# Attention, then two MLPs, on one core: block 0's first two pairs ahead of block 1, its x written from PSUM, and an order that knows the shared port

## The chip, the cores and the metric

The kernel runs on one core of a Trainium2 chip. TensorE multiplies, VectorE, ScalarE and GpSimd do the elementwise work, and SyncE issues all DMAs. The metric is the device time of the core in microseconds (us), the median of several runs of the whole kernel. Engine names in the rows: PE is TensorE's matmul, PEld its weight load, DVE VectorE, ACT ScalarE, POOL GpSimd, SPq SyncE's queue.

## The reference

All inputs and the result are float32 in shape, but the values need more than half precision: several inputs are drawn with factors of 8, q with 64.

```
# attention, 8 batches, 8 heads, 576 tokens, head size 64, 32 packed queries p per head
def sm_attn(qq, kk, vv):
    s = scale * qq @ kk.T; s = s - max(s); a = exp(s); a = a / (sum(a) + 1e-9); return a @ vv
p_packed = sm_attn(p, k, v)
out = sm_attn(q, p_packed, p_packed)
x = out, heads joined: 4608 tokens x 512
# first MLP, 512 -> 1536 -> 512
x = (silu(x @ w_gate) * (x @ w_val)) @ w_out
# second MLP, 512 -> 2048 -> 512
h = x @ w_in;  g = h if h >= 1, 0 if h <= -1, else (h + 1)**2 / 4
result = g @ w_out
```

The weights arrive as float64 words and are turned into float32 on the chip.

## The kernel before, in words

Precision comes from splitting: every float32 operand is scaled by a power of two and split into a float16 high part and a float16 low part, and each product is made as three float16 products (high x low, low x high, high x high). To save products, 2 x 2 blocks of quarters are multiplied by a scheme of Strassen's kind with seven products (P1 to P7). For that, sums and differences of quarters are made first (`sums`, `split_quarters`, line 501), on GpSimd or VectorE.

The work comes in these pieces:

- Attention goes by "quads" of four heads; two quads (0 and 1) make batch 0, quads 2 and 3 batch 1, and so on to 15. A quad has `load`, `stage_a` (scores of p against k, softmax), `stage_b` (transposes, values, norms and exponents of the packed heads), `stage_c` (scores of q, softmax) and `stage_d` (outputs, evacuated from PSUM, scaled and stored in the DRAM tensor `xT`). The last quad of a batch also makes `kx1`, an exponent for the batch's x.
- The tokens are cut into nine blocks of 512. Block 0 lies in batch 0; block 1 takes the last 64 tokens of batch 0 and most of batch 1. `load_x` (line 1187) brings a block's x in as two `raw` tiles, `split_x` scales and splits it and also stores the split form (`xsp`); `fetch_x` reads that form again when another pair needs it.
- The first MLP's hidden layer goes in six "pairs" of unit tiles. A unit (`first_unit`, 84 products of 256 columns at line 1110) makes one pair's hidden values for one block; the products with the output weights follow, at line 1248 for pairs 0 to 2 (`second_products`, 24 products of 512 columns per pair and block) and at line 1366 for the rest. The second MLP has eight units and the same two steps.
- `PHASES` (line 552) sets the order of units: pair 0 for blocks 0 and 1, pair 1 for blocks 0 and 1, pair 2 for blocks 0 and 1, then pairs 0 to 2 for the other blocks, then pairs 3 to 5 for all.
- Weights are converted (`convert_w1`, `prepare_w1`, `convert_chunk`, `prepare_w2`): the words are joined (`from_words`), the values are squared, a matmul with ones sums the squares over the partitions, VectorE takes the maximum over the columns, and from it come an exponent and a scale.

What sets the order of instructions is a planner written out in Python, the class `Order` (line 42). Each operation is registered with an estimated cost on every engine that can do it, its reads, writes and buffers. A simulation then picks, for each engine that is free, the waiting operation with the earliest due time ("late", from the order in which TensorE's work is registered) whose inputs are there and whose buffers can be had. TensorE's own work is taken nearly as registered, from a window of 32. The instructions are issued in that order; on the chip each engine works through its own list and waits where an input is missing. Buffers come from pools (38 `op`, 4 `raw`, 8 PSUM banks `ps`, 4 `h`), and those of the main pools are handed out in the order of registration. An operation marked `shared` is one that VectorE and GpSimd can't do at the same time, in the planner's model.

Around the first units, places (two per unit) say when what is registered: `NEXT` for the quads, `LATE` for the weights of pairs 1, 2 and so on, `CHUNKS` for those of the second MLP. `load(i)` takes two `op` buffers for k and two for v.

Of the kernel before, what the change touches and what calls it, by code (L numbers as in the profile page):

```python
# [9 lines left out]
F32 = mybir.dt.float32  # L10
# [32 lines left out]
class Order:  # L43
# [8 lines left out]
    PATIENCE = {"exp": 0.0}  # L52
    WINDOW = 32
# [72 lines left out]
    def run(self):  # L126
# [126 lines left out]
def packed_attention_then_two_mlps(ctx, tc, qT, kT, v, pT, w1, wo, w2, wo2, out):  # L253
# [52 lines left out]
    a2s = const.tile([128, 2 * U2], I32, name="a2s")  # L306
    top1 = const.tile([128, U1 + G1], F32, name="top1")
# [5 lines left out]
    kp = const.tile([128, B * NQUAD, 3], I32, name="kp")  # L313
# [187 lines left out]
    def split_quarters(raw, scale, op, key, left, wait_sum=0.0, wait_lo=0.0):  # L501
        base = lambda: raw.t[:, 0:4, :]
        copy(1024, base, base, q(raw, 0, 1, 2, 3) + [key], q(raw, 0, 1, 2, 3), scale=scale)
# [14 lines left out]
    def sums(raw, left, wait):  # L518
# [14 lines left out]
        (1, (0, 1), (0, 2)), (1, (1, 2), (0, 2)), (1, (2, 3), (0, 2)), (1, (0, 3), (2, NB)), (1, (3, 6), (0, NB)),  # L533
# [60 lines left out]

    def convert_w1(item):
# [3 lines left out]
        for src in srcs:  # L599
# [5 lines left out]
            for a, b in ((0, 512), (512, 1024)):  # L605
                wb = o.buf("h")
                n = b - a

                def words(wb=wb, n=n):
                    return wb.t.rearrange("p a b n -> p (a b n)").bitcast(I32).rearrange("p (n w) -> p n w", w=2)  # L610

                dma(n * 0.001, words,
                    lambda src=src, a=a, b=b: src[:, a:b].bitcast(I32).rearrange(
                        "p (n w) -> p n w", w=2),
                    [], [(wb, 0)])
                dst = lambda a=a, b=b, line=line: line()[:, a:b]
                from_words(words, dst, [(wb, 0)], q(raw, *range(a // N, (b - 1) // N + 1)), n)
# [4 lines left out]
    def prepare_w1(item):  # L622
        kind, p = item
        raws = st.pop(("w1", item))
        ps = o.buf("ps")

        def norm():
            for u, (_, sq) in enumerate(raws):
                s = sq()
                if kind == "out":  # L630
                    moving, dst = [s[:, 0:4:3, :], s[:, 1:3, :]], ps.t
                else:
                    moving = [m[:, :, h:h + 128] for m in (s[:, 0:4:3, :], s[:, 1:3, :])
                              for h in (0, 128)]
                    dst = ps.t[:, u * 256:u * 256 + 256]
                for m, mv in enumerate(moving):
                    nc.tensor.matmul(dst, ones, mv, start=(m == 0), stop=(m == len(moving) - 1))  # L637

        pe(0.43 * len(raws), norm, [k for raw, _ in raws for k in q(raw, 4, 5)], [(ps, 0)],
           unit=ps, opens=True)  # L640
        i = p if kind == "in" else U1 + p
        dve(512, lambda: nc.vector.tensor_reduce(top1[:, i:i + 1], ps.t[:, :512], axis=AX.X, op=ALU.max),
            [(ps, 0)], [("top", 1, i)], 1.5, 0.0)
# [14 lines left out]
    def load(i):  # L658
        b, qd = divmod(i, NQUAD)
        pb = o.buf("pb")  # L660
        kt, vt = [o.buf("op") for _ in range(2)], [o.buf("op") for _ in range(2)]
# [7 lines left out]
        for j, c0, c1 in ((0, 0, 3), (1, 3, 4)):  # L669
            dma(0.2, lambda j=j, c0=c0, c1=c1: flat(vt[j], (c1 - c0) * 4 * D).rearrange(  # L670
                "p (c d) -> p c d", d=4 * D
            ), lambda c0=c0, c1=c1: v[b, 128 * c0:128 * c1, cols].rearrange("(c p) d -> p c d", p=128),
                [], [(vt[j], 0)])
        dma(0.1, lambda: flat(vt[1], 8 * D)[:S - 512, 4 * D:], lambda: v[b, 512:, cols],
            [], [(vt[1], 1)])
        st["in", i] = (kt, vt, pb)
# [28 lines left out]
    def stage_a(i):  # L705
        kt, vt, pb = st["in", i]
# [22 lines left out]
    def stage_b(i):  # L729
        b, qd = divmod(i, NQUAD)  # L730
        vt = st.pop(("in", i))[1]
# [24 lines left out]
        def values():  # L756
            for c, (off, n) in enumerate(CH):
                vc = flat(vt[c // 3], 768)[:n, (c % 3) * 4 * D:]
# [6 lines left out]
        pe(0.92, values, [(a1T, 0), (a1T, 1), (vt[0], 0), (vt[1], 0), (vt[1], 1)], [(pv, 0)],  # L765
# [58 lines left out]
        if qd == NQUAD - 1:  # L824
# [4 lines left out]
            field(lambda: kx1[:, b:b + 1], lambda: topx[:, b:b + 1], [("topx", b)], [("kx1", b)], 2.0)  # L829
        st[i] = (pp, parts, ppT)  # L830

    def stage_c(i):
# [33 lines left out]
        z2 = o.buf("op")  # L866
# [4 lines left out]
        copy(S, lambda: halves(0), lambda: flat(z, S), [(z, 0)], [(z2, 0)])  # L871
# [4 lines left out]
    def stage_d(i):  # L876
        b, qd = divmod(i, NQUAD)
        pp, parts, z2, halves = st.pop(i)
        for j in range(2):
            xs = o.buf("op")  # L880
            for u in range(2):
# [10 lines left out]
                copy(H2, lambda u=u, xs=xs: flat(xs, S)[:, u * H2:(u + 1) * H2],  # L892
                     lambda xo=xo: xo.t[:, :H2], [(xo, 0), ("kp", i, 2)], [(xs, u)], 1.0,
                     scale=lambda: kp[:, i, 2:3].bitcast(F32), psum=True)
            dma(0.3, lambda j=j: xT[:, 2 * qd + j, b * S:(b + 1) * S], lambda xs=xs: flat(xs, S),
                [(xs, 0), (xs, 1)], [("x", b, qd, j)], 10.0)
            if b == 0:
                st["xs", qd, j] = xs
# [233 lines left out]
    def convert_chunk():  # L1132
# [14 lines left out]
        square(512, sq, dst, q(b, "d"), q(b, "w"))  # L1147
        dma(0.25, lambda: w2f[:, i, 512 * h:512 * h + 512], dst, q(b, "d"), [("w2f", i, h)])
        t = o.buf("ps")
        n = 128 if i < U2 else 512  # L1150

        def norm():
            for m in range(512 // n):
                nc.tensor.matmul(
                    t.t[:, :n], ones, sq()[:, m * n:(m + 1) * n],
                    start=(m == 0), stop=(m == 512 // n - 1),
                )

        pe(0.25, norm, q(b, "w"), q(t, 0), unit=t, opens=True)

        dve(n, lambda: nc.vector.tensor_reduce(
            top2[:, i, h:h + 1], t.t[:, :n], axis=AX.X, op=ALU.max
        ), q(t, 0), [("top", 2, i, h)], 1.5, 0.0)
        if h == 1 and i % 2 == 1:

            j = i - 1
            dve(1, lambda: nc.vector.tensor_reduce(
                top2[:, j, 0:1], top2[:, j:j + 2, :], axis=AX.XY, op=ALU.max
            ), [("top", 2, j + u, c) for u in range(2) for c in range(2)], [("top", 2, j, 0)], None, 0.0)
# [17 lines left out]
    def load_x(layer, b):  # L1187
        src = {1: xT, 2: x2T}[layer]
        raws = []
        for kk in range(2):  # L1190
            raw = o.buf("raw")
            for kh, sl in ((0, slice(0, 2)), (1, slice(2, 4))):
                halves = lambda kk=kk, kh=kh: src[:, kk + 2 * kh, b * T:(b + 1) * T]
                if layer == 1 and b == 0:
                    xs = st.pop(("xs", kh, kk))
                    halves, r = lambda xs=xs: flat(xs, S)[:, :T], [(xs, 0), (xs, 1)]
                elif layer == 2:
# [9 lines left out]
    def split_x(layer, b, pw, raws):  # L1207
        out_ops = []
        for d, raw in enumerate(raws):
            op = operand()  # L1210
            split_quarters(raw, pw.x(), op, (pw.f, 0), False, SUM_WAIT, X_LO)
# [170 lines left out]
    def total(b):  # L1382
        t = o.buf("ps")
        pe(0.1, lambda: nc.tensor.matmul(t.t[:, :4], ones32, sq2[:, b, :]),
           [("sq2", b)], [(t, 0)], unit=t, opens=True)

        dve(4, lambda: nc.vector.tensor_reduce(
            topx[:, B + b:B + b + 1], t.t[:, :4], axis=AX.X, op=ALU.add
        ), [(t, 0)], [("topx2", b)], 2.0, 0.0)
# [210 lines left out]
    for k, (n, p) in enumerate(line):  # L1600
# [94 lines left out]
```

## Time and profile before

| | |
|---|---|
| runs | 1619.83, 1624.52, 1621.31 us, median 1621.31 |
| profiled execution | 1620.46 us, span 1618.7 us |
| mean granted clock of TensorE | 0.984 |
| DMA traffic | 308.60 MB on the program's queue |
| chain that ended last | PE 85%, DVE 7%, ACT 2%, issue 2%, POOL 2%, DMA 1% |

The span runs from the first to the last instruction. Busy times are sums over an engine's instructions; an idle time in brackets in a row of the timeline is the time the engine stood still ahead of the row, with the instruction that ended it.

### The profile page before, as it was taken

The numbers are of one execution on the slowest core, as the hardware profiler recorded it, in microseconds if no ns is written. First come the engines' busy times: TensorE is split into PE (matmuls) and PEld (weight loads), VectorE is DVE, ScalarE is ACT, GpSimd is POOL, SyncE is SP. The second block draws the span as 40 slices with busy tenths as digits, with TensorE's granted clock in tenths as the row PEclk, the third lists the DMA queues.
The fourth block names the chain that finished last, engine by engine and source line by source line (L and its number), as shares of the span: only waits on it lengthen the run. The fifth ranks groups of instructions, "written<-read, shape, count | busy, mean of one in ns | idle before, by whom it ended". The sixth has DMA issues, their size and how long they took to land.

```text
span 1618.7 us, 35291 instructions
## 1 busy us (share of the span) xinstructions
PE 1555.6 (96%) x13772; PEld 1290.2 (80%) x13772; DVE 1298.2 (80%) x2104; ACT 989.4 (61%) x1690; POOL 1167.4 (72%) x993
## 2 busy tenths in 40 slices
PE   4778999999999999999999999999999999999999
PEld 2446666776777778888888888888888888888888
DVE  8889998778675647889999899988777898775674
ACT  5767677677665456666666767666554556654541
POOL 5476556475464357778769989988788888886884
PEclk8779999999999999999999999999999999999999
DMA  8776967647337755666776853245433553244422
GB/s 295 244 268 234 334 223 238 199 170 236 133 140 250 265 179 194 233 249 234 262 238 207 303 190 128 102 150 189 160 105 121 186 182 119 102 170 160 150 60 79
DMA packets 147240, 310.86 MB, mean 192 GB/s; under 512 B 18560, under 2 KB 55424, under 8 KB 147072
## 3 DMA queue, kind: packets, MB, share of 16 engines
q1 hardware_dynamic: 147072, 308.60, 55.7%
q8 instruction: 108, 1.77, 0.4%
q14 instruction: 60, 0.49, 0.1%
HBM read 191.76 MB, written 115.74 MB: 190 GB/s over the span
## 4 chain that ended last, share of the span: by engine, by line
PE 85%; DVE 7%; ACT 2%; issue 2%; POOL 2%; DMA 1%; SPq 0%; POOLq 0%; DVEq 0%; ACTq 0%
PE ps L1110 46%; PE ps L1366 27%; PE ps L1248 7%; PE ps L697 2%; PE ps L886 1%; POOL op L364 1%; POOL raw L364 1%; DVE raw L364 1%; DVE raw L438 1%; DVE h L434 1%; DVE ps L1093 0%; ACT op L376 0%; DMA x2T<-acc 0%; DVE h L1093 0%; PE ps L637 0%
## 5 line engine op out<-in xcount | busy, mean ns | idle before, releaser
L1110 PE MATMUL ps<-op,op 128*128 128x256 f16 x7560 | 906.2, 273 | 7.0 <-DVE u L382 2.5
L1110 PEld LDWEIGHTS <-op 128*128 128x128 f16 x7560 | 737.7, 98 | 116.6 <-issue 14.5
L364 POOL TENSOR_TENSOR op<-h,op 128x512 f16<-128x512 f32 (+2 forms) x344 | 419.5, 1238 | 167.0 <-ACT op L376 140.6
L1366 PE MATMUL ps<-op,op 128*128 128x256 f16 x4158 | 513.3, 273 | 0.0
L1366 PEld LDWEIGHTS <-op 128*128 128x128 f16 x4158 | 406.7, 98 | 47.5 <-issue 0.3
L376 ACT CAST op<-h 128x512 f16<-128x512 f32 (+2 forms) x368 | 202.9, 591 | 92.0 <-POOL h L364 36.1
L364 POOL TENSOR_TENSOR raw<-raw 128x256 f32<-128x256 f32 (+1 forms) x169 | 156.2, 938 | 71.0 <-ACT raw L378 43.4
L364 POOL TENSOR_TENSOR h<-h,h 128x512 f32<-128x512 f32 (+1 forms) x160 | 197.9, 1237 | 11.9 <-DVE h L1488 4.3
L1485 ACT ACTIVATE ps<-m,half,f 128x512 f32<-128x512 f32 x144 | 112.3, 780 | 108.0 <-POOL m L1482 61.1
L378 ACT ACTIVATE p<-ps,f 128x512 f32<-128x512 f32 x174 | 118.8, 685 | 95.2 <-PE ps L1110 90.2
L1266 DVE SCALAR_TENSOR_TENSOR acc<-ps,f,acc 128x512 f32<-128x512 f32 x169 | 125.7, 744 | 58.6 <-PE ps L1366 55.8
L364 POOL TENSOR_TENSOR op<-raw,op 128x512 f16<-128x512 f32 (+3 forms) x100 | 157.3, 1593 | 15.7 <-ACT op L376 9.5
L1248 PE MATMUL ps<-op,op 128*128 128x512 f16 x648 | 155.4, 379 | 0.0
L1488 DVE SCALAR_TENSOR_TENSOR h<-ps,f,h 128x512 f32<-128x512 f32 x144 | 106.4, 742 | 32.5 <-ACT ps L1485 32.3
L1093 DVE SCALAR_TENSOR_TENSOR h<-ps,f,p 128x512 f32<-128x512 f32 x126 | 93.5, 743 | 42.5 <-PE ps L1110 37.2
L1248 PEld LDWEIGHTS <-op 128*128 128x128 f16 x648 | 63.0, 98 | 57.2 <-issue 0.9
L364 POOL TENSOR_TENSOR h<-h 128x512 f32<-128x512 f32 x57 | 78.1, 1371 | 26.0 <-DVE h L1457 15.3
L1482 POOL TENSOR_SCALAR m<-h,f 128x512 f32<-128x512 f32 x72 | 61.7, 856 | 48.6 <-ACT ps L1485 28.9
L364 DVE TENSOR_TENSOR op<-h,op 128x512 f16<-128x512 f32 (+1 forms) x79 | 96.7, 1234 | 0.0
L364 POOL TENSOR_TENSOR op<-op,t 128x576 f32<-128x576 f32 x32 | 39.9, 1246 | 71.9 <-DVE t L848 22.5
L378 ACT ACTIVATE u<-ps,f 128x512 f32<-128x512 f32 x87 | 59.6, 685 | 44.9 <-PE ps L1110 44.6
L376 ACT CAST op<-raw 128x512 f16<-128x512 f32 (+3 forms) x126 | 77.5, 655 | 13.9 <-DVE raw L364 6.9
(148 smaller groups left out, 1791.2 us busy)
## 6 DMA issues: line engine op xcount, KB each, us to landing
op<-xsp SPq DMA_DIRECT2D x88, 448.0 KB, 6.2
xsp<-op SPq DMA_DIRECT2D x72, 448.0 KB, 4.2
sums<-acc SPq DMA_DIRECT2D x88, 256.0 KB, 2.7
acc<-sums SPq DMA_DIRECT2D x88, 256.0 KB, 3.6
op<-wsp SPq DMA_DIRECT2D x44, 448.0 KB, 4.8
op<-wsp_out SPq DMA_DIRECT2D x38, 448.0 KB, 5.3
h<-in_w SPq DMA_DIRECT2D x24, 512.0 KB, 5.2
op<-in_kT SPq DMA_DIRECT2D x32, 288.0 KB, 5.3
```

The costliest lines, as they stand in the source:

```text
L364: lambda e: engine(e).tensor_tensor(dst(), x(), y(), op=op), r, w, late,
L376: nc.scalar.copy(dst(), src())
L378: nc.scalar.activation(dst(), src(), AF.Copy, scale=scale())
L697: nc.tensor.matmul(ps.t[64 * j:64 * j + 64, :H2], left(j), flat(right[j], S)[:, u * H2:(u + 1) * H2])
L1093: psum_dve(T, lambda: nc.vector.scalar_tensor_tensor(dst(), lanes(bank.t), self.r(), lanes(add.t), op0=ALU.mult, op1=ALU.add), [(bank, 0), ...
L1110: nc.tensor.matmul(dst, a, b, start=start, stop=stop, skip_group_check=True)
L1248: nc.tensor.matmul(bank.t, x[:, js], y, start=first and i == 0 and m == 0, stop=last and i == 1 and m == 2,)
L1266: psum_dve(T, lambda: nc.vector.scalar_tensor_tensor(acc.t, bank.t, pw.output()(), acc.t, op0=ALU.mult, op1=ALU.add), r + [(acc, 0)], [(ac ...
L1366: nc.tensor.matmul(bank.t[:, l * N:(l + 1) * N], x, y, start=first and l == 0 and m == 0, stop=last and l == 1 and m == 2, skip_group_chec ...
L1482: o.add({"POOL": 0.85, "DVE": 0.42}, lambda e: engine(e).tensor_scalar(out=lanes(m.t), in0=dst(), scalar1=top(), scalar2=low(), op0=ALU.mi ...
L1485: act(T, lambda: nc.scalar.activation(bank.t, m.t, AF.Square, bias=half_one[:, 0:1], scale=inv()), [(m, 0), (f, 0)], [(bank, 0)], fixed=0.35)
L1488: psum_dve(T, lambda: nc.vector.scalar_tensor_tensor(dst(), lanes(bank.t), top(), dst(), op0=ALU.mult, op1=ALU.max), [(bank, 0), (h, t), ( ...
```

## The change

- `PHASES`: block 0 takes pairs 0 and 1, then block 1 takes them; pair 2 follows for both. `LATE` and `NEXT` are set for it: pair 1's weights are due half to two places earlier, the quads 2 to 5 half to one place later.
- Block 0's x is evacuated from PSUM into the two `raw` tiles directly, with one scale that holds the quad's and the block's exponent (`kp[..., 3]`, from `kpx`). The DMA from `xs` to `raw` and the scaling of 1024 columns go; of batch 0 only the last 64 tokens go to `xT`.
- The split x of blocks 0 and 1 stays in its buffers for pairs 1 and 2 instead of being fetched again.
- The norms of the output weights are whole sums: ScalarE's squares sum over the columns (`squares`), a small matmul sums over the partitions, and `sum_of` adds the columns. Before, the maximum over columns was taken.
- v lies beside k in three `op` buffers per quad, and `z2` uses the buffer of `zt`.
- The planner: VectorE puts off a shared operation while the port is held for more than 0.1 us, if another is ready that isn't due more than 5 us later; SyncE issues no DMA while more than 4 us of transfers are queued; TensorE's costs count 1.18 times in the first 140 us. For the first three units x of the next unit, not the next but one, is prepared.

```diff
+    QUEUED = 4.0
+    EARLY = 140.0, 1.18
+    PORT, AHEAD = 0.1, 5.0
...
-                end = now + op.costs[eng]
+                end = now + op.costs[eng] * (self.EARLY[1] if eng == "PE" and now < self.EARLY[0] else 1.0)
...
-                skipped = []
+                if eng == "SP" and channel - now > self.QUEUED:
+                    upcoming.append(channel - self.QUEUED)
+                    continue
+                skipped, second = [], None
...
+                    if second and op.late > second.late + self.AHEAD:
+                        skipped.append(item)
+                        break
                     if wait > now:
                         upcoming.append(wait)
                     elif self.obtainable(op):
-                        start(op, eng)
-                        break
+                        if eng == "DVE" and op.shared and port - now > self.PORT:
+                            second = second or op
+                        else:
+                            second = None
+                            start(op, eng)
+                            break
                     skipped.append(item)
+                if second:
+                    start(second, eng)
...
-        copy(1024, base, base, q(raw, 0, 1, 2, 3) + [key], q(raw, 0, 1, 2, 3), scale=scale)
+        if scale is not None:
+            base = lambda: raw.t[:, 0:4, :]
+            copy(1024, base, base, q(raw, 0, 1, 2, 3) + [key], q(raw, 0, 1, 2, 3), scale=scale)
...
-        (1, (0, 1), (0, 2)), (1, (1, 2), (0, 2)), (1, (2, 3), (0, 2)), (1, (0, 3), (2, NB)), (1, (3, 6), (0, NB)),
+        (1, (0, 1), (0, 1)), (1, (1, 2), (0, 1)), (1, (0, 1), (1, 2)), (1, (1, 2), (1, 2)), (1, (2, 3), (0, 2)), (1, (0, 3), (2, NB)), (1, (3, 6), (0, NB)),
...
+    def squares(src, keys, acc, key):
+        act(512, lambda: nc.scalar.activation(junk, src(), AF.Square, accum_out=acc), keys, [key], fixed=0.25)
+    def sum_of(cols, keys, dst, key):
+        t, n = o.buf("ps"), cols.shape[-1]
+        pe(0.1, lambda: nc.tensor.matmul(t.t[:, :n], ones32, cols), keys, [(t, 0)], unit=t, opens=True)
+        dve(n, lambda: nc.vector.tensor_reduce(dst, t.t[:, :n], axis=AX.X, op=ALU.add),
+            [(t, 0)], [key], 1.5, 0.0)
...
-        kt, vt = [o.buf("op") for _ in range(2)], [o.buf("op") for _ in range(2)]
+        kt = [o.buf("op") for _ in range(3)]
...
+            if b == 0:
+                power(lambda: kpx, lambda: kx1[:, 0:1], -1.0, 202.0, [("kx1", 0)], [("kpx", 0)], 2.0)
+                dve(NQUAD, lambda: nc.vector.tensor_scalar_mul(
+                    kp[:, :NQUAD, 3].bitcast(F32), kp[:, :NQUAD, 2].bitcast(F32), kpx.bitcast(F32)
+                ), [("kpx", 0), *(("kp", j, 2) for j in range(NQUAD))],
+                    [("kp", j, 3) for j in range(NQUAD)], 2.0, 0.0)
...
-        z2 = o.buf("op")
+        z2 = zt
...
+                lo, hi = u * H2, (u + 1) * H2
+                if b == 0:
+                    n = min(hi, T) - lo
+                    copy(n, lambda line=line, lo=lo, n=n: line()[:, lo:lo + n],
+                         lambda xo=xo, n=n: xo.t[:, :n], [(xo, 0), ("kp", i, 3)],
+                         q(raw, *range(2 * qd + u, 2 * qd + 2)), 1.0,
+                         scale=lambda: kp[:, i, 3:4].bitcast(F32), psum=True)
+                    lo = max(lo, T)
...
+    NEAR = 3
-    LATE = (1, 2, 5, 6, 14, 26, 38, 43, 48, 52)
+    LATE = (0, 0.5, 5, 7, 14, 26, 38, 43, 48, 52)
-    NEXT, SPACE, AHEAD = (0, 0.5, 1.2, 3.4, 6, 8.5, 11), 2.8, 1
+    NEXT, SPACE, AHEAD = (0.2, 0.9, 1.9, 3.9, 6, 8.5, 11), 2.8, 1
...
+        if layer == 1 and b == 0:
+            return [st.pop(("x", j)) for j in range(2)]
...
-            if pairs[0] > 0:
+            if (layer, b, (0, 1)) in xops and pairs[0] < PLAIN:
+                xops[key] = xops[layer, b, (0, 1)]
+            elif pairs[0] > 0:
                 xops[key] = fetch_x(layer, b)
...
-                if k + 2 < len(line):
-                    block_x(*parts[line[k + 2][0]])
+                then = k + (1 if k < NEAR else 2)
+                if then < len(line):
+                    block_x(*parts[line[then][0]])
```

## Rows read from the trace of the kernel before

**Rows 1.** The page: the span, and busy time of each engine (share, instructions).

```profile
span 1618.7 us, 35291 instructions
PE 1555.6 (96%) x13772; PEld 1290.2 (80%) x13772; DVE 1298.2 (80%) x2104; ACT 989.4 (61%) x1690; POOL 1167.4 (72%) x993
```

**Rows 2.** Busy time by stretch: start:end, length, engines, granted clock, DMA share, GB/s.

```profile
0.00:70.70 70.70, 37.42 (x303) 19.86 (x304) 57.21 (x185) 43.26 (x92) 39.19 (x40) 0.76 0.77 258
70.70:83.20 12.50, 12.50 (x109) 10.09 (x109) 10.98 (x31) 8.64 (x15) 2.87 (x3) 0.98 1.01 356
83.20:140.00 56.80, 42.72 (x355) 29.52 (x353) 49.55 (x102) 38.22 (x67) 36.87 (x30) 0.85 0.75 256
140.00:300.00 160.00, 152.85 (x1358) 109.15 (x1357) 147.14 (x304) 114.91 (x213) 100.05 (x81) 1.00 0.76 256
300.00:1618.70 1318.70, 1310.12 (x11654) 1121.53 (x11652) 1033.28 (x1485) 784.36 (x1305) 988.44 (x842) 1.00 0.51 176
```

**Rows 3.** Timeline of TensorE at norm products: start, duration, line, operands, count.

```profile
475.84 0.59 PE L637 MATMUL ps<-raw,ones 128*128 128x512 bf16 x2
476.27 2.78 PE L1110 MATMUL ps<-op,op 128*128 128x256 f16 x24
...
649.50 0.38 PE L1154 MATMUL ps<-raw,ones 128*128 128x512 bf16 x1
649.72 1.47 PE L1110 MATMUL ps<-op,op 128*128 128x256 f16 x12
...
644.78 0.28 PE L1384 MATMUL ps<-sq,ones 128*128 128x4 f32 x2
644.92 0.82 PE L1366 MATMUL ps<-op,op 128*128 128x256 f16 x6
```

**Rows 4.** Timelines of four engines ahead of the first unit.

```profile
36.56 0.14 DVE L444 TENSOR_SCALAR kx<-topx 128x1 int32<-128x1 int32 x1
39.88 0.48 ACT L378 ACTIVATE op<-ps,kp 128x288 f32<-128x288 f32 x1
49.52 3.06 PE L886 MATMUL ps<-op,op 128*128 128x288 f16 x12
51.17 0.50 ACT L378 ACTIVATE op<-ps,kp 128x288 f32<-128x288 f32 x1 [0.22 <-PE ps L886]
56.93 1.15 ACT L378 ACTIVATE raw<-raw,f 128x1024 f32<-128x1024 f32 x1 [0.17 <-DMA raw<-op]
57.05 1.33 POOL L364 TENSOR_TENSOR op<-op,t 128x576 f32<-128x576 f32 x1 [8.41 <-DVE t L848]
58.34 2.88 POOL L364 TENSOR_TENSOR raw<-raw 128x512 f32<-128x512 f32 x3
70.59 5.72 PE L1110 MATMUL ps<-op,op 128*128 128x256 f16 x48
```

**Rows 5.** Timelines of ScalarE and TensorE: pair 1's weights and the second unit.

```profile
53.97 1.07 ACT L391 ACTIVATE raw<-raw 128x1024 bf16<-128x1024 f32 x1
78.33 1.05 PE L637 MATMUL ps<-raw,ones 128*128 128x256 bf16 x8
96.57 5.35 PE L1248 MATMUL ps<-op,op 128*128 128x512 f16 x24
114.80 11.16 PE L1110 MATMUL ps<-op,op 128*128 128x256 f16 x96
```

**Rows 6.** Timelines of GpSimd and VectorE: the same small operation, twice.

```profile
47.10 1.54 POOL L364 TENSOR_TENSOR op<-op,op 128x576 f16<-128x576 f32 x1 [2.31 <-PE ps L741]
47.42 1.25 DVE L1042 TENSOR_SCALAR f<-f 128x5 f32<-128x5 f32 x1
72.03 0.17 DVE L1042 TENSOR_SCALAR f<-f 128x5 f32<-128x5 f32 x1
```

**Rows 7.** The page's DMA issues (count, size, landing) and one of TensorE's waits.

```profile
op<-in_kT SPq DMA_DIRECT2D x32, 288.0 KB, 5.3
...
PE ps L697 <- DMA pb<-in_pT: 10.8, 1, 10.8
```

More of the change, by code (lines that the diff above doesn't have):

```diff
@@ L306, in packed_attention_then_two_mlps @@
     a2s = const.tile([128, 2 * U2], I32, name="a2s")
+    sq1 = const.tile([128, G1, 2], F32, name="sq1")
+    sqw2 = const.tile([128, U2, 2], F32, name="sqw2")
     top1 = const.tile([128, U1 + G1], F32, name="top1")
@@ L312, in packed_attention_then_two_mlps @@
     topx = const.tile([128, B + NB], F32, name="topx")
-    kp = const.tile([128, B * NQUAD, 3], I32, name="kp")
+    kp = const.tile([128, B * NQUAD, 4], I32, name="kp")
+    kpx = const.tile([128, 1], I32, name="kpx")
     sq2 = const.tile([128, NB, 4], F32, name="sq2")
@@ L616, in convert_w1 @@
                 dst = lambda a=a, b=b, line=line: line()[:, a:b]
-                from_words(words, dst, [(wb, 0)], q(raw, *range(a // N, (b - 1) // N + 1)), n)
+                keys = q(raw, *range(a // N, (b - 1) // N + 1))
+                from_words(words, dst, [(wb, 0)], keys, n)
+                if kind == "out":
+                    squares(dst, keys, sq1[:, p, a // n:a // n + 1], ("sq1", p, a // n))
+            if kind == "out":
+                st["w1", item].append((raw, None))
+                continue
             sq = lambda raw=raw: raw.t[:, 4:6, :].bitcast(BF16).rearrange("p a (b n) -> p (a b) n", b=2)
@@ L624, in prepare_w1, with norm @@
         raws = st.pop(("w1", item))
[L625 to L640, printed above, removed]
-        i = p if kind == "in" else U1 + p
-        dve(512, lambda: nc.vector.tensor_reduce(top1[:, i:i + 1], ps.t[:, :512], axis=AX.X, op=ALU.max),
-            [(ps, 0)], [("top", 1, i)], 1.5, 0.0)
+        i = p if kind == "in" else U1 + p
+        if kind == "out":
+            sum_of(sq1[:, p, :], [("sq1", p, m) for m in range(2)], top1[:, i:i + 1], ("top", 1, i))
+        else:
+            ps = o.buf("ps")
+            def norm():
+                for u, (_, sq) in enumerate(raws):
+                    s = sq()
+                    moving = [m[:, :, h:h + 128] for m in (s[:, 0:4:3, :], s[:, 1:3, :]) for h in (0, 128)]
+                    for m, mv in enumerate(moving):
+                        nc.tensor.matmul(ps.t[:, u * 256:u * 256 + 256], ones, mv, start=(m == 0), stop=(m == 3))
+            pe(0.43 * len(raws), norm, [k for raw, _ in raws for k in q(raw, 4, 5)], [(ps, 0)],
+               unit=ps, opens=True)
+            dve(512, lambda: nc.vector.tensor_reduce(top1[:, i:i + 1], ps.t[:, :512], axis=AX.X, op=ALU.max),
+                [(ps, 0)], [("top", 1, i)], 1.5, 0.0)
         field(lambda: k1[:, i:i + 1], lambda: top1[:, i:i + 1], [("top", 1, i)], [("k", 1, i)])
@@ L668, in load, with values_at @@
         cols = slice(4 * qd * D, 4 * (qd + 1) * D)
[L669 to L676, printed above, removed]
+        for c, (off, n) in enumerate(CH):
+            if c in (3,):
+                continue
+            g = 2 if c == 2 else 1
+            dma(0.13 * g if n == 128 else 0.1, lambda c=c, n=n, g=g: values_at(kt, c, g)[:n],
+                lambda off=off, n=n, g=g: v[b, off:off + n * g, cols].rearrange("(c p) d -> p c d", p=n),
+                [], [(kt[min(c, 2)], 1 + (c == 4))])
+        st["in", i] = (kt, pb)
+    def values_at(kt, c, n=1):
+        if c < 2:
+            return flat(kt[c])[:, S:S + 4 * D].unsqueeze(1)
+        return flat(kt[2], 3 * 4 * D).rearrange("p (c d) -> p c d", d=4 * D)[:, c - 2:c - 2 + n, :]
     def load_q(i):
@@ L763, in values @@
                     )
-        pe(0.92, values, [(a1T, 0), (a1T, 1), (vt[0], 0), (vt[1], 0), (vt[1], 1)], [(pv, 0)],
+        pe(0.92, values, [(a1T, 0), (a1T, 1), (kt[0], 1), (kt[1], 1), (kt[2], 1), (kt[2], 2)], [(pv, 0)],
            unit=pv, opens=True)
@@ L1146, in convert_chunk, with norm @@
         from_words(words, dst, q(b, "w"), q(b, "d"), 512)
-        square(512, sq, dst, q(b, "d"), q(b, "w"))
+        if i < U2:
+            square(512, sq, dst, q(b, "d"), q(b, "w"))
+        else:
+            squares(dst, q(b, "d"), sqw2[:, i - U2, h:h + 1], ("sq2w", i, h))
         dma(0.25, lambda: w2f[:, i, 512 * h:512 * h + 512], dst, q(b, "d"), [("w2f", i, h)])
[L1149 to L1163, printed above, removed]
+        if i < U2:
+            t = o.buf("ps")
+            def norm():
+                for m in range(4):
+                    nc.tensor.matmul(
+                        t.t[:, :128], ones, sq()[:, m * 128:(m + 1) * 128], start=(m == 0), stop=(m == 3),
+                    )
+            pe(0.25, norm, q(b, "w"), q(t, 0), unit=t, opens=True)
+            dve(128, lambda: nc.vector.tensor_reduce(
+                top2[:, i, h:h + 1], t.t[:, :128], axis=AX.X, op=ALU.max
+            ), q(t, 0), [("top", 2, i, h)], 1.5, 0.0)
         if h == 1 and i % 2 == 1:
             j = i - 1
-            dve(1, lambda: nc.vector.tensor_reduce(
-                top2[:, j, 0:1], top2[:, j:j + 2, :], axis=AX.XY, op=ALU.max
-            ), [("top", 2, j + u, c) for u in range(2) for c in range(2)], [("top", 2, j, 0)], None, 0.0)
+            if i < U2:
+                dve(1, lambda: nc.vector.tensor_reduce(
+                    top2[:, j, 0:1], top2[:, j:j + 2, :], axis=AX.XY, op=ALU.max
+                ), [("top", 2, j + u, c) for u in range(2) for c in range(2)], [("top", 2, j, 0)], None, 0.0)
+            else:
+                sum_of(sqw2[:, j - U2:i - U2 + 1, :].rearrange("p a b -> p (a b)"),
+                       [("sq2w", j + u, c) for u in range(2) for c in range(2)], top2[:, j, 0:1],
+                       ("top", 2, j, 0))
             field(lambda: k2[:, j:j + 1], lambda: top2[:, j, 0:1], [("top", 2, j, 0)], [("k", 2, j)])
@@ L1193, in load_x @@
                 halves = lambda kk=kk, kh=kh: src[:, kk + 2 * kh, b * T:(b + 1) * T]
[L1194 to L1197, printed above, removed]
+                if layer == 2:
                     r = [("x2", b, i) for i in range(4)]
@@ L1210, in split_x @@
             op = operand()
-            split_quarters(raw, pw.x(), op, (pw.f, 0), False, SUM_WAIT, X_LO)
+            scale = None if layer == 1 and b == 0 else pw.x()
+            split_quarters(raw, scale, op, (pw.f, 0), False, SUM_WAIT, X_LO)
             for h in range(2):
@@ L1382, in total @@
     def total(b):
[L1383 to L1389, printed above, removed]
+        sum_of(sq2[:, b, :], [("sq2", b)], topx[:, B + b:B + b + 1], ("topx2", b))
         field(lambda: kx2[:, b:b + 1], lambda: topx[:, B + b:B + b + 1], [("topx2", b)], [("kx2", b)])
```

28 lines of the change are left out of this document (16 added, 12 removed).

## Prediction

> **What bounds the kernel now.** I read the page first [rows 1]: TensorE is busy 96% of the span, so what can be won is either TensorE work or the 63 us in which it is idle (1618.7 less 1555.6). Then the busy time by stretch [rows 2] shows where those 63 us lie: 33.3 before the first product of the first MLP layer at 70.7 us, none up to 83.2, 14.1 from there to 140, 7.2 from 140 to 300, and 8.6 in the 1319 us that remain, the draining of the output among them. So there are two kinds of place. From 140 us on TensorE is the bound, and only work taken off it counts. Before 140 us it waits for operands that the other engines make: VectorE is busy 57.2 of the first 70.7 us and 49.6 of the 56.8 us from 83.2 to 140, the granted clock of TensorE is 0.76 and 0.85 there, so part of that time is spent at 1.2 GHz, and the DMA engines are busy three quarters of the time. What is moved there is worth the wait that it ends, unless VectorE, still busy 147.1 of the 160 us up to 300, gives it back.
>
> **The sum** is made against the profiled execution, 1620.46 us (span 1618.7 and 1.8 around it). The median of the runs is 1621.31, 0.85 above it; I add that at the end.
>
> **A. Norms of the output weights.** Per pair of the first layer two 512-column products go. In the full stretch such a pair holds TensorE for 0.43 us, from its start to the start of the product behind it (475.84 to 476.27). For each of the 16 half tiles of the second layer's output weights one goes, at 0.22 (649.50 to 649.72) [rows 3]. Pairs 2 to 5 lie where TensorE is full: 4 x 0.43 = 1.7, and 16 x 0.22 = 3.5; pairs 0 and 1 lie in the idle time and count nothing here. In their place come 4 + 4 whole sums over 2 or 4 columns. The kernel has that product already, for x of the second layer: 644.78 to 644.92, so 0.14 each, or 1.1 for eight. A = -4.1. If each kept TensorE for its whole recorded 0.28 us it would be -3.0, and with the sums free -5.2. The squares were made by ScalarE already and stay there with an accumulator read behind each; ScalarE is busy 784 of the last 1319 us, which hides it. Should a weight come late for it, TensorE waits; such waits are among the 8.6 us.
>
> **B. x of block 0 from PSUM.** Quad 1's outputs leave TensorE from 49.52, and ScalarE evacuates them, the second of four from 51.17 to 51.67. Then come a DMA from tile to tile and a scaling of 1024 columns, which starts for the first half at 56.93; GpSimd's sums of quarters start at 58.34 and the first product at 70.59 [rows 4]. The change writes the scaled values straight into that buffer. The second evacuation then completes the first half; with a short piece for the store between, I put that at 52.0. GpSimd was idle for the 8.4 us ahead of 57.05. So its sums can start 58.34 - 52.0 = 6.3 us earlier, and the 12.3 us from there to the first product stay. B = -6.3. Ends: -8.4, all of that idle time, and 0, if the steps of quads 2 and 3 take the gap. What is added: two operations of one and two columns on VectorE ahead of quad 0's evacuations, whose input is there at 36.7, 3 us before the first of these at 39.88, and four evacuations of the last 64 columns, behind the ones that matter. Off the path both cost nothing; with that cover gone, 4 x 0.5 = 2 us at the length of the larger evacuation. The block's store to xT shrinks to 64 columns.
>
> **C. Block 0 takes pair 1 before block 1.** The squares of pair 1's input weights ended at 55.0, but their norm stood in TensorE's order at 78.33, behind the first unit; the unit that uses them started at 114.80 [rows 5] (I take it for block 0's, since block 1's x was still being split). Ahead of it stood the steps of quads 2 to 4, each waiting for its own chain. With the new order the norm stands ahead of the first unit, so the scaling and splits behind it can run in GpSimd's idle time, and 84 products (9.8 us at the 11.16 of 96 from 114.80) and then 24 of the second kind (5.35 us, as those from 96.57) lie where the 14.1 us of waits are. Block 1's x gets that much more cover. I take 8 of the 14.1; ends 0 and -14.1. What is late next is block 1's x, which needs quads 2 and 3; their steps b and d move one place back, and VectorE has to do them all the same. Keeping x on chip removes 16 fetches of 448 KB (two blocks, two pairs, four each); TensorE's waits name no fetch, so I count 0 for it (above 0, if the buffers held are missed: a rival below).
>
> **D. The port-aware order.** In the trace a five-element operation of VectorE took 1.25 us from 47.42, ending with GpSimd's 1.54 us operation from 47.10; the same one took 0.17 at 72.03 [rows 6]. So an operation of the one engine waits for one of the other to end. Choosing another operation meanwhile returns some of that, but only what TensorE waits for counts: 7.2 us in 140 to 300, of which I take -2; ends -7 and +3 (a new order makes waits of its own; 3 is a fifth of the 15.8 us that TensorE is idle after 140 us now). The changed estimates of early TensorE steps and the held-back DMA issues act only through the order and go in here, as do three input buffers per quad instead of four with one DMA more each (16 more issues on a queue whose DMAs land in 5.3 us and are started ahead).
>
> The Trainium skill (SBUF — State Buffer, section "SBUF: two separate sides") says that the port pair of VectorE and GpSimd is an exclusive lock for the whole instruction, taken by VectorE for operations in a two-port mode or with two inputs in SBUF. The trace agrees in the 1.25 us, and the operation concerned is one that the new order does not mark as shared. By that rule an unmarked operation put in front is blocked just as well and D would be 0, and the sum 2 us more.
>
> **E. Given back.** What is ahead at 140 us, about 14 us, has to be kept up by VectorE with 13 us idle in the next 160. The quads run well ahead of their blocks, so much can slide. I take +4; ends 0 and +14.
>
> Sum: 1620.5 - 4.1 - 6.3 - 8 - 2 + 4 = 1604.1, and 0.85 for the median: **1605.0**.
>
> **Rivals.**
> *All early gains are given back.* VectorE is the bound up to 300 us and TensorE only waits elsewhere: for it the 92% of 140 to 300, against it that its waits there sum to 7.2 us. Only A stays: 1620.5 - 4.1 + 0.85 = 1617.3.
> *More is won.* B at its end, C whole, D at -5, nothing returned: 1620.5 - 4.1 - 8.4 - 14.1 - 5 + 0.85 = 1589.8. For it the low clock of 0.85 up to 140 us, which a TensorE without waits there might not see; against it VectorE's 87% in that stretch.
> *Slower: the operand pool runs dry.* x of blocks 0 and 1 holds 8 of 38 buffers until pair 2 is through, and buffers are given out in the order of the program, so a quad's load waits for them. A quad's first product, which stands in TensorE's order, then waits for its transfer; such a DMA lands in 5.3 us, and the one wait of TensorE for an input's transfer at that product is the first of all, 10.8 us [rows 7]. Each late quad costs 5.3; the sum of 16.4 is used up by three, and with four or five of quads 4 to 8 the time is 1605 + 4.5 x 5.3 = 1629. For it: 16 more buffers belong to the weights of three pairs in this stretch (12 of input, 4 of output). Against it: block 0's four x tiles, one value buffer per quad and one of step c go, and the fetched copies held as many before while they were in use.
> *It does not do what it says*: the order that is planned puts pair 1 later all the same. Then A and B stay, 1620.5 - 4.1 - 6.3 + 0.85 = 1611, inside the forecast's range; it goes with the forecast.
>
> **Chances.** Forecast 0.50, more won 0.18, given back 0.20, slower 0.12. A measurement of this kernel can tell about 0.3%, 4.9 us, from no change. The given-back case at 1617 is half inside that, so faster is 0.50 + 0.18 + 0.10 = 0.78, the same 0.10, slower 0.12. The range from 1588 to 1622 takes in the first three cases but for the edge below 1588, and leaves out the slower one.
>
> **What would show it.** B: the first product of the first layer near 64 us and no scaling of 1024 columns ahead of it. C: 84 more products and 24 of the second kind done by 105 us, and idle time of some 6 us between the end of the first unit and 140. A: the 512-column norm products gone, TensorE's busy time lower by 3 to 5 us. D: VectorE's small operations shorter on the mean. E: idle time from 140 to 300 above 7.2 us. The forecast is wrong if a quad's first product waits for a transfer more than twice, if the stretch from 140 to 300 takes back over 10 us, or if the stretch after 300 has over 12 us idle.

## The result and the profile after

The changed kernel takes 1604.61 us (median; 1603.73 to 1604.91) against 1620.57 of the kernel before: a ratio of 0.9897, or 16 to 17 us, with an interval of 0.9878 to 0.9915, or 14 to 20 us. The forecast was 1605.0. The profiled execution is 1604.35 us with a span of 1602.4, so 16.1 below the one that the sum was made against. The time is right; several of the steps to it are not, as the rest shows.

Page of the changed kernel, the rows that answer to [rows 1]:

```profile
span 1602.4 us, 35228 instructions
PE 1548.6 (97%) x13764; PEld 1290.2 (81%) x13764; DVE 1276.6 (80%) x2079; ACT 990.5 (62%) x1730; POOL 1163.9 (73%) x996
```

TensorE's idle time fell from 63.1 to 53.8 us, its busy time by 7.0. Busy time by stretch, to be held against [rows 2] (the first row spans their first two); columns are start:end, length, busy time of PE, PEld, DVE, ACT and POOL with counts, granted clock, DMA share, GB/s:

```profile
0.00:83.20 83.20, 50.19 (x413) 30.54 (x414) 72.50 (x230) 55.78 (x119) 45.45 (x46) 0.83 0.74 248
83.20:140.00 56.80, 47.76 (x387) 32.42 (x388) 49.91 (x103) 41.51 (x79) 27.45 (x23) 0.90 0.59 202
140.00:300.00 160.00, 154.62 (x1393) 113.21 (x1391) 142.87 (x296) 117.06 (x223) 99.27 (x80) 1.00 0.69 233
300.00:1602.40 1302.40, 1296.04 (x11577) 1113.98 (x11575) 1011.30 (x1452) 776.20 (x1312) 991.75 (x849) 1.00 0.52 178
```

TensorE's idle time, the length of a stretch less PE's busy time, is 33.0 us up to 83.2 (33.3 before), 9.0 up to 140 (14.1), 5.4 up to 300 (7.2) and 6.4 behind that (8.6). So the first stretch, in which the first unit comes much earlier, has no less idle time. Its timeline on TensorE (start, duration, line, operands, count, idle time ahead) shows where that went:

```profile
54.74 0.61 PE L1174 MATMUL ps<-op,op 128*128 128x256 f16 x4
55.66 6.56 PE L1174 MATMUL ps<-op,op 128*128 128x256 f16 x56 [0.30 <-POOL op L384]
63.17 1.47 PE L1174 MATMUL ps<-op,op 128*128 128x256 f16 x12 [0.95 <-ACT u L398]
64.47 0.60 PE L674 MATMUL ps<-raw,ones 128*128 128x256 bf16 x4
66.44 0.60 PE L674 MATMUL ps<-raw,ones 128*128 128x256 bf16 x4 [1.37 <-ACT raw L411]
68.67 0.58 PE L623 MATMUL ps<-sq,ones 128*128 128x2 f32 x2 [1.63 <-ACT junk L618]
...
70.24 2.72 PE L1174 MATMUL ps<-op,op 128*128 128x256 f16 x12
...
83.05 1.38 PE L783 MATMUL ps<-ident,op 128*128 128x128 f32 x5 [3.51 <-ACT op L760]
```

The first product comes at 54.74, 15.9 us earlier than in [rows 4], and the first unit ends at 72.96. Pair 1's norms (L674, L623) now stand behind the unit's sixth step and wait there for their squares, and the second unit's first products follow only at 87.16, against 114.80 in [rows 5].

To see what a lead is worth I count the products done up to a time, here units and second products at 140 and 300 us (same columns, TensorE's instructions of one line alone), before:

```profile
0.00:140.00 140.00, 29.32 (x252) 0.82 0.78 266
0.00:300.00 300.00, 111.59 (x952) 0.91 0.77 261
...
0.00:140.00 140.00, 5.35 (x24) 0.82 0.78 266
0.00:300.00 300.00, 46.37 (x198) 0.91 0.77 261
```

and after:

```profile
0.00:140.00 140.00, 33.62 (x259) 0.85 0.68 229
0.00:300.00 300.00, 120.42 (x996) 0.93 0.68 231
...
0.00:140.00 140.00, 11.66 (x48) 0.85 0.68 229
0.00:300.00 300.00, 50.90 (x210) 0.93 0.68 231
```

Counted with the attention's scores, values and outputs, each at the spacing of its kind at 2.4 GHz (0.109 us a product of 256 columns, 0.216 of 512, 0.137 an output, 0.128 a score, 0.021 a value), this gives the lead over the kernel before, in us of TensorE's work. The other rows are experiments below.

```
up to (us)                  83.2   140   200   250   300   500   700
changed kernel               0.0   6.5   4.6   4.6   9.0  11.2  13.0
without the planner part     0.0   6.0   1.5   0.4  -1.7  -1.2   0.5
planner part alone          -0.4   5.4  -0.2   0.4   1.9   1.6   1.7
order of pairs undone        0.0   3.2   2.4   2.5   4.2   5.3   6.9
first product held back     -0.7   3.2   2.4   2.1   5.5   7.5   9.5
port part alone undone       0.0   6.0   2.5   2.6   5.8   4.6   6.3
held-back DMAs undone        0.0   8.5   3.2   2.6   4.5   4.1   5.9
control, delay 0.13         -0.5   7.9   2.8   3.3   7.4   9.6  10.9
control, kernel before       0.0   3.4   2.2  -1.2   0.8   2.5   2.6
more marked as shared        0.0   1.9   0.9  -1.2  -1.7  -0.2   1.7
```

At 83.2 us the lead is nothing, at 140 it is 6.5 (24 more second products are 5.2 of it), and it is more at 300 and 700. Of the 6.5, 5.3 are less idle time; the rest is more counted work in the same busy time, in which the norm products of two pairs are gone and the granted clock was 0.85 against 0.82. A lead in one plan is not a steady quantity: the control on the kernel before, in which nothing but a constant of the planner differs, has 3.4 us at 140 and ends 2 us slower.

### The profile page after: what moved, and what is told of

It reads as the page before. It is cut to its first block, busy times and chain, and to the rows that moved or that the text cites. A ratio compares the mean times of both kernels' runs of the same rounds, so it can differ in the third digit from the quotient of the medians.

```text
span 1602.4 us, 35228 instructions
## 1 busy us (share of the span) xinstructions
PE 1548.6 (97%) x13764; PEld 1290.2 (81%) x13764; DVE 1276.6 (80%) x2079; ACT 990.5 (62%) x1730; POOL 1163.9 (73%) x996
## 4 chain that ended last, share of the span: by engine, by line
PE 88%; DVE 6%; ACT 2%; DMA 2%; issue 1%; POOL 0%; SPq 0%; DVEq 0%; ACTq 0%; POOLq 0%
PE ps L1174 48%; PE ps L1436 27%; PE ps L1318 8%; PE ps L739 2%; DVE op L384 1%; PE ps L940 1%; DMA h<-in_wo 1%; ACT op L396 1%; DVE h L1157 1%; PE ps L802 0%; DVE raw L458 0%; POOL op L384 0%; DMA pb<-in_pT 0%; DMA raw<-xT 0%; DVE h L1552 0%
## 5 line engine op out<-in xcount | busy, mean ns | idle before, releaser
L384 POOL TENSOR_TENSOR op<-h,op 128x512 f16<-128x512 f32 (+2 forms) x340 | 409.2, 1222 | 152.9 <-ACT op L396 140.5
L384 POOL TENSOR_TENSOR raw<-raw 128x256 f32<-128x256 f32 (+1 forms) x166 | 161.4, 985 | 71.6 <-ACT raw L398 65.6
L384 POOL TENSOR_TENSOR h<-h,h 128x512 f32<-128x512 f32 (+1 forms) x156 | 189.0, 1211 | 8.1 <-DVE op L384 3.7
L384 POOL TENSOR_TENSOR h<-h 128x512 f32<-128x512 f32 x62 | 83.3, 1343 | 33.6 <-DVE h L1521 18.8
L1546 POOL TENSOR_SCALAR m<-h,f 128x512 f32<-128x512 f32 x79 | 66.2, 838 | 50.2 <-ACT ps L1549 32.3
L384 DVE TENSOR_TENSOR op<-h,op 128x512 f16<-128x512 f32 (+1 forms) x83 | 93.2, 1132 | 2.1 <-POOL h L384 1.1
L396 ACT CAST op<-raw 128x512 f16<-128x512 f32 (+3 forms) x132 | 84.9, 683 | 5.4 <-POOL raw L384 3.0
```

Source lines behind the costliest of these rows:

```text
L384: lambda e: engine(e).tensor_tensor(dst(), x(), y(), op=op), r, w, late,
L396: nc.scalar.copy(dst(), src())
L1546: o.add({"POOL": 0.85, "DVE": 0.42}, lambda e: engine(e).tensor_scalar(out=lanes(m.t), in0=dst(), scalar1=top(), scalar2=low(), op0=ALU.mi ...
```

## The experiments

Four undo one part of the change, then come two controls and two parts of the planner, then two experiments in the changed kernel's own order, one part alone, and one extension. The edits are shown shortened. Differences to the changed kernel are those of the ratios to the kernel before, times 1621 us; each is uncertain by 3 to 5 us.

**Norms undone.**

```diff
-    squares(dst, keys, sq1[:, p, a // n:a // n + 1], ("sq1", p, a // n))
+    square(1024, sq, ...); matmul(dst, ones, mv, ...) over 512 columns; tensor_reduce(..., op=ALU.max)
```

> The changed kernel with the norms of the output weights as before (maxima over columns, 512-column products), all else as changed. By the sum of the prediction TensorE gets back 16 x 0.22 + 4 x 0.43 us and loses eight sums of 0.14: the time is 1604.6 + 4.1 = 1608.7 us, and the idle time of TensorE after 300 us stays near the changed kernel's 6.4. By the rival, that the norms were free because the order hides them and the gain lies in the early order alone, 1604 to 1606.

1616.14 us, ratio 0.997 (0.9959 to 0.9981): 11.8 above the changed kernel, more than either reading. The first product came at 58.79.

**Order of pairs and blocks undone.**

```diff
-    PHASES (0, 1),(0, 1) / (1, 2),(0, 1) / (0, 1),(1, 2) / (1, 2),(1, 2);  NEAR = 3;  LATE = (0, 0.5, 5, 7, ...);  NEXT = (0.2, 0.9, 1.9, 3.9, ...)
+    PHASES (0, 1),(0, 2) / (1, 2),(0, 2);  LATE = (1, 2, 5, 6, ...);  NEXT = (0, 0.5, 1.2, 3.4, ...)
```

> The changed kernel with the order of pairs and blocks as before (pair 0 for blocks 0 and 1, then pair 1), with the due places of weights and quads and the look-ahead of before. By the prediction's term C 8 us come back: 1612 us, the first product still near 55 us. By the rival that the early lead of 16 us is lost up to 140 us whatever the order, at most 1607.

1611.48 us, 0.9947 (0.9932 to 0.9962): 8.1 back. That is the number of term C, but not its price: the first product came at 66.67, so this part, and not x from PSUM alone, makes the early start, and undoing it takes away much of B's lead too:

```profile
66.67 2.77 PE L1173 MATMUL ps<-op,op 128*128 128x256 f16 x12
```

**x from PSUM undone.**

```diff
-    copy(n, line, xo, scale=kp[:, i, 3:4])            # PSUM to raw
+    copy(H2, xs, xo, scale=kp[:, i, 2:3]); dma(raw, xs); copy(1024, raw, raw, scale=pw.x())
```

> The changed kernel with block 0's x brought from tile to tile by DMA and scaled over 1024 columns as before. By the prediction's term B the first product of the first MLP comes about 6 us later than the changed kernel's 54.7, near 61, and the whole time is 1604.6 + 6.3 = 1611 us. By the rival that VectorE bounds up to 300 us and takes the lead back, the first product comes as late but the time is 1604 to 1606.

1614.43 us, 0.9961 (0.9947 to 0.9976): 10.4 back. One product ran at 59.65; the rest of the first unit waited, and its main run came 9.8 us after the changed kernel's 55.66:

```profile
64.38 0.80 PE L1151 MATMUL ps<-op,op 128*128 128x256 f16 x3 [4.46 <-POOL op L383]
65.46 8.67 PE L1151 MATMUL ps<-op,op 128*128 128x256 f16 x68 [0.29 <-DVE op L383]
```

**Planner undone.**

```diff
-    QUEUED = 4.0;  EARLY = 140.0, 1.18;  PORT, AHEAD = 0.1, 5.0   # and what uses them
```

> The changed kernel with the planner of before (no putting off for the port, no held-back DMA issue, TensorE's early costs as before). By the prediction's term D 2 us come back: 1606.6 us, the first product near 55 to 57 us. By the rival that the planner made most of the early lead (quad 1's outputs left TensorE 4.7 us earlier, which the prediction did not have), the first product is at 60 us or later and the time 1612 us or more.

1624.21 us, 1.0019 (1.0008 to 1.003): 19.8 back, slower than the kernel before although every other part is in. The first product came at 55.95, so the rival's time came true but its reason, that the planner makes the early start, did not. The lead table shows what is lost: the 6.0 us at 140 are all given back by 300, and TensorE is idle 11.2 us in between. The longest of TensorE's waits up to 140 us (total, times, longest), but for the first input, name the whole sum of an output weight, which stood in its order ahead of its squares:

```profile
PE ps L607 <- ACT junk L602: 9.9, 2, 8.2
PE ps L767 <- ACT op L744: 8.0, 3, 3.8
```

They lie ahead of 140 us, where this run had its lead all the same, so they don't explain the loss behind it. There, up to 300 us, no single wait stands out; the longest are:

```profile
PE ps L1158 <- DVE op L368: 2.5, 1, 2.5
PE ps L825 <- ACT junk L793: 2.5, 3, 1.2
```

**Two controls.** These four losses sum to 50 us where the whole gain is 16.7, so they can't be four prices. The controls change nothing but a constant of the planner.

```diff
-    LAG = 0.12
+    LAG = 0.13
```

> A control: the changed kernel with the planner's assumed delay between an operation and those that wait for it at 0.13 instead of 0.12 us. The work is the same to the last instruction kind; only ties in the planned order fall differently. If the single edits carry the gain, the time stays within 3 us of the changed kernel's 1604.6. If instead the planned order is so sensitive that any edit costs several us, so that the losses of the undone parts (7 to 20 us, 48 in sum against a whole gain of 16) are mostly loss of a favourable order, it is 1610 us or more, and the undone parts can't be read as prices.

1611.22 us, 0.9929 (0.9907 to 0.9952): 5.2 above the changed kernel.

> The same control on the kernel before: 0.13 instead of 0.12 us of assumed delay. If the order of the kernel before is as sensitive, the time is 1625 us or more; if only single edits count, within 3 us of the 1621.3 of the kernel before on this chip.

1624.33 us, 1.0013 (1.0004 to 1.0022): 2 us above the kernel before. So two arbitrary shifts of the plan cost 2 and 5 us, and of each undone part that much, and perhaps more, is no price of the part. The two single planner parts can't be told from it:

```diff
-    PORT, AHEAD = 0.1, 5.0
+    PORT, AHEAD = 1e9, 5.0
```

> The changed kernel without the putting off of shared operations on VectorE; held-back DMA issues and early TensorE costs stay as changed. By the prediction's term D 2 us come back, 1606.6. By the theory that the planner's port part made the early lead, the first product comes at 60 us or later and the time is 1615 us or more, most of the 19.6 us that the whole planner's undoing cost.

1613.58 us, 0.9944 (0.9927 to 0.9961): 7.6 back, first product at 58.59.

```diff
-    QUEUED = 4.0
+    QUEUED = 1e9
```

> The changed kernel without the held-back DMA issue of the planner; the rest as changed. By the prediction no part of its own: 1603 to 1607. By the rival that the loss without the whole planner part (TensorE waited 8.2 us for the squares of an output weight) comes from the order of the DMAs, 1612 us or more and that wait shows again.

1612.83 us, 0.9942 (0.9926 to 0.9959): 7.3 back.

**Norm products put back in the changed kernel's own order.** An instruction that the planner does not cost leaves the order as it is, so this measures term A without the control's blur.

```diff
+            for _ in range(more):      # 8 at a sum over 2 columns, 16 at one over 4
+                nc.tensor.matmul(t.t[:, :512], ones, ones.unsqueeze(1).broadcast_to([128, 4, 128]), start=True, stop=True)
```

> The changed kernel in its own planned order, to the instruction, with the products that the norms of the output weights cost before put back four times over (dummy products of 512 columns: 8 at each of the six sums of the first layer, 16 at each of the four of the second) ahead of each whole sum. Only TensorE's work differs, so the order can't blur it. If the norm products lay on the path where TensorE is full, as the prediction's term A has it, the time grows by 4 x (3.5 + 1.7) = 20.8 us, up to 24 with the two sums in the idle stretch: 1625 to 1629, so that taking them off once is worth 5.2 less the sums' 1.1. If waits hid them, by less than 10.

1625.57 us, 1.0026 (1.0017 to 1.0036): 20.9 more, against 20.8 expected. Each burst shows as it was priced, 16 products from 666.37 to 669.82 and 8 from 465.48 to 467.21:

```profile
666.37 3.62 PE L627 MATMUL ps<-ones 128*128 128x512 bf16 x16
669.82 0.28 PE L628 MATMUL ps<-sqw,ones 128*128 128x4 f32 x2
...
465.48 1.89 PE L627 MATMUL ps<-ones 128*128 128x512 bf16 x8
467.21 0.28 PE L628 MATMUL ps<-sq,ones 128*128 128x2 f32 x2
```

**First product held back, in the changed kernel's own order.**

```diff
+                if not delayed:
+                    delayed.append(True)
+                    for _ in range(64):
+                        nc.tensor.matmul(bank.t[:, :N], ones, ones.unsqueeze(1).broadcast_to([128, 2, 128]), start=True, stop=True)
```

> The changed kernel in its own planned order with 64 dummy products of 256 columns (7 us at full clock, 14 at half) on TensorE right ahead of the first product of the first MLP layer. It takes back part of the 15.9 us by which that product came earlier. By the prediction (the lead counts, little is given back) the time grows by nearly as much as the first product is later: 7 to 12 us, 1612 to 1616. By the theory that the early lead is worth less than half, because block 1's x and VectorE's work set the pace up to 140 us (the lead of 15.9 at the first product was about 6 at 137 us), by 2 to 5 us: 1607 to 1610.

TensorE's timeline shows the 64 products and the unit behind them:

```profile
54.92 7.16 PE L1173 MATMUL ps<-ones 128*128 128x256 bf16 x64
61.92 6.71 PE L1180 MATMUL ps<-op,op 128*128 128x256 f16 x60
```

The first product was 7.2 us later, and the time 1609.19 us, 0.9924 (0.9909 to 0.9939): 4.4 more by the ratio, 3.8 by the profiled executions. So in this order a microsecond of lead at this point is worth about a half; by the ratio's interval, from 0.1 to 1.1. The loss is there in full at 140 us (3.2 against 6.5 in the table) and does not grow or heal. The added products also kept TensorE busy: its granted clock up to 140 us was 0.87 against 0.85, so a part of the loss may have been paid back by the clock, which no run separates.

**The planner part alone, on the kernel before.**

```diff
+    QUEUED = 4.0;  EARLY = 140.0, 1.18;  PORT, AHEAD = 0.1, 5.0   # and what uses them
```

> The kernel before with the new planner alone (port-aware, held-back DMA issue, early TensorE costs). With the three others it makes a square: neither 1621.3, the rest alone 1624.2, both 1604.6. If the planner carries the gain, 1605 to 1610 with the first product at 60 us or earlier. If planner and rest only pay together (the norms' wait, the early x), within 4 us of 1621.3. By the prediction's term D 1619.3.

1619.65 us, 0.9987 (0.9978 to 0.9996): 2 us, as term D had it, with the first product at 68.12. The square is then 1 (neither), 0.9987 (planner), 1.0019 (rest), 0.9897 (both). The two parts alone come to nothing; together they are worth 17.7 us more than their sum, over three times the larger control. The next run, however, shows that a new plan of the same work can lose nearly as much.

**More operations marked as shared.**

```diff
-    dve(n, fn, r + [(f, 0)], [(f, 0)], None, 0.15)
+    dve(n, fn, r + [(f, 0)], [(f, 0)], None, 0.15, shared=True)    # and three others like it
```

> The changed kernel with the small operations of VectorE on two inputs or scalars in on-chip memory (the exponents' and powers' columns, the scaled sums of softmax, the low part of the packed heads) marked as shared for the planner, as the trace showed them to wait for GpSimd. If the unmarked operations block the port-aware order, VectorE's waits shrink and the time falls to 1600 or below. If the order's sensitivity rules, as in the control, it lands between 1606 and 1614 although the plan is truer.

1621.11 us, 0.9994 (0.9985 to 1.0004): 15.7 worse than the changed kernel. The lead at 140 us was 1.9, and by 300 it was gone. By the Trainium skill's rule of an exclusive lock on the shared port (SBUF — State Buffer, section "SBUF: two separate sides") the small operation of [rows 6] should have gained. It did: its eighteen instances of eight columns, in the second layer, took 0.39 us on the mean against 0.81 in the changed kernel. Its six of five columns are too few to tell (0.31 here, 0.22 in the changed kernel, 0.48 in the control on it, 0.35 before). VectorE's busy time fell from 1276.6 to 1225.0 us, in part because 35 operations fewer ran on it. So the truer marking did what it was to do, and the kernel lost 15.7 us all the same: shorter port waits alone brought nothing here, and the work was the same, so the loss lies in when it is done and by which engine. The rows are the changed kernel's, the control's and this run's with its page (busy us and mean ns behind the bar):

```profile
L1106 DVE TENSOR_SCALAR f<-f 128x8 f32<-128x8 f32 x18 | 14.5, 805 | 0.3
...
L1106 DVE TENSOR_SCALAR f<-f 128x5 f32<-128x5 f32 x6 | 1.3, 222 | 0.0
```

```profile
L1106 DVE TENSOR_SCALAR f<-f 128x5 f32<-128x5 f32 x6 | 2.8, 475 | 0.0
```

```profile
L1106 DVE TENSOR_SCALAR f<-f 128x8 f32<-128x8 f32 x18 | 7.0, 391 | 0.0
...
L1106 DVE TENSOR_SCALAR f<-f 128x5 f32<-128x5 f32 x6 | 1.9, 314 | 0.0
```

```profile
PE 1556.8 (96%) x13764; PEld 1293.0 (80%) x13764; DVE 1225.0 (76%) x2044; ACT 1000.9 (62%) x1744; POOL 1182.4 (73%) x1019
```

## Why the time was right and where the steps were not

**A, -4.1: right.** The products put back four times cost 20.9 us, so 5.2 once, and 4.1 with the 1.1 us of the new sums taken off. TensorE's busy time fell by 7.0 us, more than the 3 to 5 that were named as the sign; what the rest is, no run separates. The new sums hold TensorE for 0.14 us each, as priced from [rows 3]:

```profile
660.79 0.28 PE L623 MATMUL ps<-sqw,ones 128*128 128x4 f32 x2
660.93 0.82 PE L1436 MATMUL ps<-op,op 128*128 128x256 f16 x6
```

**B, -6.3: the mechanism was there, the step to the time failed.** x came straight from PSUM; GpSimd waited for the evacuations and began at 48.20, not at 52.0:

```profile
47.67 0.84 ACT L398 ACTIVATE raw<-ps,kp 128x224 f32<-128x224 f32 x2
48.20 2.72 POOL L384 TENSOR_TENSOR raw<-raw 128x512 f32<-128x512 f32 x2 [3.41 <-ACT raw L398]
```

The first product was 15.9 us earlier rather than 6.3, since quad 1's outputs also came 4.7 us sooner (44.84 for eleven of the twelve) and the 12.3 us from the sums to the first product, which I had left as they were, became 6.5. In those 12.3 us GpSimd had done two steps of quads among those of x; now they come later:

```profile
61.18 1.34 POOL L364 TENSOR_TENSOR op<-op,t 128x576 f32<-128x576 f32 x1
...
65.81 1.46 POOL L364 TENSOR_TENSOR op<-op,op 128x576 f16<-128x576 f32 x1
```

```profile
50.89 4.72 POOL L384 TENSOR_TENSOR op<-raw,op 128x1024 f16<-128x1024 f32 x3
```

Either part undone (x or the order of pairs) puts the unit's main run back to 65 or 67 us, so the 15.9 is theirs together. But I booked the lead as time gained. TensorE spent it waiting, 3.0 us for pair 1's norms and 3.5 for quad 4's softmax among it, and stood at 83.2 where it had stood before. Held back by 7.2 us, the kernel lost about 4, so the early start isn't free to lose either.

**C, -8: half right.** The second unit came 27.6 us earlier, in pieces between the steps of quads, and the idle time from 83.2 to 140 fell by 5.0, not 8. By 105 us 72 more products and 13 of the second kind were done, where the prediction named 84 and 24, and TensorE was idle 12.7 us between the end of the first unit and 140, where it named 6. B and C together were to be 14.3 and were 6.5 at 140 us: that is the mis-sized term of the sum.

**D, -2, and E, +4: the two were not separate.** The planner alone was worth 2, as forecast, but not by the way that the prediction gave. Its sign was that VectorE's small operations become shorter on the mean. Of the operation of [rows 6] the six of five columns did (0.35 to 0.22 us), but the eighteen of eight did not: they took 0.65 us before, 0.81 in the changed kernel and 0.51 in it without the planner part:

```profile
L1042 DVE TENSOR_SCALAR f<-f 128x8 f32<-128x8 f32 x18 | 11.6, 646 | 0.3
```

```profile
L1090 DVE TENSOR_SCALAR f<-f 128x8 f32<-128x8 f32 x18 | 9.2, 510 | 0.3
```

Without the planner part the rest gives its 6.0 us back between 140 and 300, the rival "given back" to the letter; the planner alone has 5.4 us at 140 and keeps 1.9 of them. Only together the lead rises from 6.5 to 9.0 there. So D and E were -2.5 together against a forecast of +2, and by what the two parts keep the lead is not shown.

**After 300 us** 7.1 more came: 3.8 of A's 4.1 lie there (three pairs and all half tiles), and the idle time fell by 2.2. The remaining 1 is within what the runs tell. Early lead 6.5, the stretch to 300 2.5 and the rest 7.1 make the 16.1; the forecast had 14.3, -2 and 4.1, or 16.4. Steps that were off by -7.8, +4.5 and +3.0 cancelled: that the time came out within half a microsecond of the forecast is luck.

**The slower rival** did not happen: after the first 10.7 us TensorE's waits name no input transfer up to 300 us. The kernel moves 299.2 MB instead of 308.6, but keeping x was not tried alone. **Open** are which of the planner's three parts saves the lead (two undone singly cost 7.3 and 7.6 us, hardly more than the control's 5.2; the early costs were not tried alone), and how much of the 16 us is the good fit of this one plan: the control says 5, and the run with more marked as shared, in which the work is the same and only the planned order and the choice of engines differ, lost 15.7. So A is shown, while the rest of the gain belongs to this order as a whole.

## What to carry to other kernels

An earlier start of the bounding engine isn't time gained until its count of work done is ahead at a later mark; count products up to several times before booking it. Where a planner lays out the order, undoing a part replans everything, so run a control that changes nothing real, and measure single terms with instructions that the planner does not see. Two edits that each make a lead and lose it again can be worth something together, so undo and add them singly and jointly. And see whether a shorter wait is on the bounding engine's path: here a small operation of VectorE took half as long and the kernel became slower.

## What was unexpected of the hardware

A whole sum over four columns in float32 is recorded as two products of together 0.28 us but holds TensorE for 0.14, while TensorE waited up to 8.2 us for its squares where the order had it early. So a tiny product's place in the order can matter more than its length, though that run still had its lead of 6.0 us at 140.
